# Gated mix of cached attention and a channel MLP, one decode step: four row groups and a float32 selector product in the output projection, first keys on a second DMA queue

## The chip, the core and the metric

The kernel runs on one core of a Trainium2 chip. A core has TensorE (PE; PEld is its weight load), VectorE (DVE), ScalarE (ACT), GpSimd (POOL) and SyncE (SP), and 16 DMA engines that all queues share. The metric is device time in microseconds, the median of several executions. One more execution is taken with the profiler; all profile times below are of that one.

## The reference

```python
def reference(A_x, A_k_cache, A_v_cache, A_wq, A_wo, B_x, B_w1, B_b1, B_w2, B_b2, gate_w):
    x = A_x                                                # (8, 1, 448) bf16
    g = _sigmoid((x * gate_w).sum(-1, keepdims=True))
    q = (x @ wq) -> 8 x 16 heads x 256                     # wq 448 x 4096
    k, v = the last 1024 rows of the caches (8, 8, 4096, 256), each head for 2 query heads
    a = (softmax(q k^T / 16) v) @ wo                       # wo 4096 x 448
    b = gelu(layernorm(x) @ w1 + b1) @ w2 + b2             # 448 -> 1792 -> 448
    return g * a + (1 - g) * b
```

## The kernel before

All data is bf16 in memory: 77.67 MB is read, nearly all of it the keys and values in use (8 batch rows, 4 MB of each), then `wq`, `w1`, `w2`, `wo`.

**Loads.** A ring of four 4 MB places (`RING = 4`) is filled in a planned order: keys of row 0, `wq`, keys 1, values 0, keys 2, values 1 and so on, `w1`, values 7 with `w2`, `wo`. `pump` issues a load when a place is free, `done` frees one. All these loads are issued by SP (`nc.sync`, lines 128, 140, 157). The keys of row 0 come in three pieces: two of 1 MB (`cuts` (2, 1)) and one of 2 MB. `wo` comes last, in seven pieces: chunks 0-7, 8-15, 16-19, 20-23, 24-27, 28-29 and 30-31 of its 32 chunks (one chunk is 128 rows of `wo`, 448 columns). Seven small loads (`x`, the gate weights, the biases) are issued by ScalarE.

**Pools.** Tiles come from pools. Tiles that are asked for under one tag share the pool's `bufs` places, and where no tag is given the tag is the name of the variable that the tile is bound to. When the places of a tag are taken, the next tile of that tag gets the place of an earlier one, and its first writer waits until the earlier one's readers have finished; a DMA that reads a tile has finished when it reports completion. `consts` has `bufs=1`. `ring`, `ktpool`, `epool`, `work` and `spool` are used with tags on purpose (`slot`, `kt`, `B`, ...).

**Stages.** The schedule is manual: every engine works in the order of the program text. `transpose_keys(b)` turns the 16 groups of four 128-column blocks of a row's keys, by TensorE (line 353) with a copy out of PSUM by ScalarE (groups in `BY_ACT`, line 359) or VectorE (line 361). For rows after 0 the first group goes another way: `turn_blocks` has one VectorE transpose (line 323) and 16 GpSimd copies (line 331). `between` hangs steps of the row before on single groups. `gate` computes the gate, `norm` the layer norm of x and its turned form, `query` the queries; then, for each row, `scores`, `top`, `expo`, `turn`, `scale`, `bring`, `values`, `finish`, `spread`. Row 0 runs as `transpose_keys(0); gate(); norm(); query(); scores(0); top(0)`. The turned x (`turned(0, ...)`), its statistics and the square root on ScalarE (lines 215 to 238) come ahead of all that.

**The end.** `mlp_hidden` gives the 14 weight chunks `hs` of the second MLP product. `oP` holds the attention output, 32 chunks. The output sum over 14 + 32 chunks is put together so: the 14 MLP chunks and chunks 0-7 go in turn to four row groups of `A1` (PSUM rows 0, 32, 64, 96; line 624), and four VectorE adds bring them into `acc` (line 632). Chunks 8-23 go to two row groups of `A3` (line 645), the odd ones up to 19 to `side`; one add brings the side in (line 653) and two bring in the rest as `fin` (line 657). The last eight chunks go to `A2`, each as two products of 224 columns in two row groups (line 666). One add gives `res`, 40 rows with both halves (line 673), and two output DMAs, one issued by SP and one by ScalarE, write one half each (lines 676, 677).

Of the kernel before, what the change touches and what calls it, by code (L numbers as in the profile page):

```python
# [17 lines left out]
def kernel(  # L18
# [27 lines left out]
    QD = 4  # L46
# [15 lines left out]
    CB = 4  # L62
    UR = NG * rep
    HALF = D // 2
    J8 = Dh // BL
    NQW = Hq // QD
    HS = NCK * Dh
    SLOT = NG * HS
    RING = 4
    EARLY = 8  # L70
    SIDE = 20
    TAIL = 8
    qscale = float(Dh) ** -0.5

    xf = A_x.rearrange("b s d -> (b s) d")
# [37 lines left out]
    def kv_loader(src, b, cuts=(1, 1), inner=False):  # L113
        pieces = [
            (i, k, cuts[i])
            for i in range(NG)
            for k in range(cuts[i])
        ]
        if inner:
            pieces.sort(key=lambda x: x[1])  # L120

        def load(t):
            for i, k, m in pieces:
                v = src[b, i * QD : (i + 1) * QD, kv_base:Sk, :].rearrange(
                    "a (s c) d -> s a (c d)", c=NCK
                )
                n = HS // m
                nc.sync.dma_start(
                    t[:, i * HS + k * n : i * HS + (k + 1) * n],
                    v[:, :, k * n : (k + 1) * n],  # L130
                )

        return load
# [71 lines left out]
    E = consts.tile([P, W + BL], F32)  # L205
    nc.gpsimd.memset(E[:, W:], 0.0)
    nc.gpsimd.memset(xs[1][:], 0.0)
    acc = consts.tile([NB, D], F32)
    fin = consts.tile([2 * BL, HALF], F32)
    nc.gpsimd.memset(fin[:], 0.0)  # L210
    oP = consts.tile([P, J8, NQW, NB], BF16)

    def turned(a, src):
# [13 lines left out]
                xw[BL * i : BL * (i + 1), a, :, BL : BL + NB], xt[:, :, i, 0:NB]  # L227
            )

    turned(0, x_sb[:])  # L230
    stats = consts.tile([NB, nc.vector.BN_STATS_DIM], F32)
    nc.vector.bn_stats(stats[:], x_sb[:])
    mv = consts.tile([NB, nc.vector.BN_AGGR_DIM], F32)
    nc.vector.bn_aggr(mv[:], stats[:])
    eps_t = consts.tile([NB, 1], F32)
    nc.vector.memset(eps_t[:], 1e-5)
    rstd = consts.tile([NB, 1], F32)
    nc.scalar.activation(rstd[:], mv[:, 1:2], ACT.Sqrt, bias=eps_t[:], scale=1.0)

    perm = consts.tile([P, P], BF16)  # L240
    mask = consts.tile([P, QD, rep], F32)
    gall = consts.tile([P, NB], F32)
    oall = consts.tile([P, NB], F32)
    b2s = consts.tile([NB, D], F32)
    b1_b = consts.tile([P, FQ], BF16)

    def gate():
        bc = consts.tile([BL, 2, D], BF16)
        nc.vector.stream_shuffle(
            bc[:].rearrange("p a d -> p (a d)"),  # L250
            rows_r[:].rearrange("p a d -> p (a d)"),
            [0] * BL,
        )
        prod = consts.tile([NB, D], F32)
        gl = consts.tile([NB, 1], F32)
        nc.vector.scalar_tensor_tensor(
            prod[:],
            in0=x_sb[:],
            scalar=1.0,
            in1=bc[0:NB, 0, :],  # L260
            op0=ALU.mult,
            op1=ALU.mult,
            accum_out=gl[:],
        )
        gth = consts.tile([NB, 1], F32)
        nc.scalar.activation(gth[:], gl[:], ACT.Tanh, scale=0.5)
        nc.vector.tensor_copy(
            perm[:].rearrange("p (s a) -> p s a", a=QD),
            ident[:].rearrange("p (a s) -> p s a", a=QD),
        )  # L270
        for r in range(rep):
            nc.vector.reduce_sum(
                mask[:, :, r], ident[:].rearrange("p (s a) -> p a s", a=QD), axis=AXIS.X
            )
        g32 = consts.tile([BL, BL], F32)
        nc.vector.memset(g32[:], 0.0)
        nc.vector.tensor_scalar(
            g32[0:NB, 0:1], gth[:], 0.5, 0.5, op0=ALU.mult, op1=ALU.add
        )
        om = consts.tile([NB, 1], F32)  # L280
        nc.vector.tensor_scalar(om[:], gth[:], -0.5, 0.5, op0=ALU.mult, op1=ALU.add)
        gt = consts.tile([BL, BL], F32)
        nc.vector.transpose(gt[:], g32[:])
        gb = consts.tile([BL, BL], F32)
        nc.vector.stream_shuffle(gb[:], gt[:], [0] * BL)
        for i in range(QD):
            nc.vector.tensor_copy(gall[BL * i : BL * (i + 1), :], gb[:, 0:NB])
        nc.vector.tensor_scalar(oall[:], gall[:], -1.0, 1.0, op0=ALU.mult, op1=ALU.add)
        nc.vector.tensor_scalar_mul(b2s[:], bc[0:NB, 1, :], om[:])

    def norm():
        nc.vector.reciprocal(rstd[:], rstd[:])
# [43 lines left out]
    def transpose_keys(b, between=None):  # L336
        between = between or {}
        kn = slot("k", b)[:].bitcast(F32)
        for hh in range(NG):
            kt = ktpool.tile([P, QD, NCK, SK, NJ], BF16, tag="kt", name="kt")  # L340
            KT[hh] = kt
            for i in range(NCK // CB):
                g = hh * (NCK // CB) + i
                if g == 0 and b > 0:
                    turn_blocks(kn, kt, 0)
                    for step in between.get(g, ()):
                        step()
                    continue
                ktp = ps_kt.tile([P, CB, P, NJ], BF16, tag="ktp", name="ktp")
                words = ktp[:].bitcast(F32)  # L350
                for c in range(CB):
                    o = (hh * NCK + i * CB + c) * P
                    nc.tensor.transpose(  # L353
                        words[:, c, :, 0], kn[:, o : o + P], ident_f[:]
                    )
                dst = kt[:, :, i * CB : (i + 1) * CB, :, :]
                src = ktp[:].rearrange("p c (s a) t -> p a c s t", a=QD)
                if g in BY_ACT:
                    nc.scalar.copy(dst, src)  # L359
                else:  # L360
                    nc.vector.tensor_copy(dst, src)  # L361
                for step in between.get(g, ()):
                    step()
        done()
# [208 lines left out]
    def steps(b):  # L573
# [8 lines left out]
        if b >= 1:  # L582
            d[9] = [lambda: finish(b - 1)]
            d[12] = [lambda: spread(b - 1)]
        return d

    transpose_keys(0)
    gate()
    norm()
    query()  # L590
    scores(0)
    top(0)
    for b in range(1, NB):
# [14 lines left out]
    spread(b)  # L608

    A1 = ps_misc.tile([P, D], F32, tag="misc", name="A1")  # L610
    A2 = ps_kt.tile([2 * BL, HALF], F32, tag="ktp", name="A2")
    A3 = ps_kt.tile([P, D], F32, tag="ktp", name="A3")
    nc.vector.memset(A2[:], 0.0)
    w2 = slot("w12")
    w = slot("wo")
    NCH = NQW * J8
    early = [(hs[:, c, :], w2[:, OW2 + c * D : OW2 + (c + 1) * D]) for c in range(FB)]
    chunks = [
        (oP[:, c % J8, c // J8, :], w[:, c * D : (c + 1) * D]) for c in range(NCH)
    ]  # L620
    early += chunks[0:EARLY]
    for i, (lhsT, rhs) in enumerate(early):
        g = i % QD
        nc.tensor.matmul(
            A1[BL * g : BL * g + NB, :],
            lhsT=lhsT,
            rhs=rhs,
            start=(i < QD),
            stop=(i >= len(early) - QD),
        )  # L630
    for g in range(QD):
        nc.vector.tensor_tensor(
            acc[:],
            A1[BL * g : BL * g + NB, :],
            acc[:] if g else b2s[:],
            op=ALU.add,
        )
    LAST = NCH - TAIL
    side = [c for c in range(EARLY, SIDE) if c % 2]
    main = [c for c in range(EARLY, LAST) if c not in side]  # L640
    res = consts.tile([2 * BL, HALF], BF16)
    for c in range(EARLY, LAST):
        mine, base = (side, 2 * BL) if c in side else (main, 0)
        lhsT, rhs = chunks[c]
        nc.tensor.matmul(  # L645
            A3[base : base + NB, :],
            lhsT=lhsT,
            rhs=rhs,
            start=(c == mine[0]),
            stop=(c == mine[-1]),  # L650
        )
        if c == side[-1]:
            nc.vector.tensor_tensor(
                acc[:], A3[2 * BL : 2 * BL + NB, :], acc[:], op=ALU.add
            )
    for h in range(2):
        nc.vector.tensor_tensor(
            fin[BL * h : BL * h + NB, :],
            A3[0:NB, h * HALF : (h + 1) * HALF],
            acc[:, h * HALF : (h + 1) * HALF],  # L660
            op=ALU.add,
        )
    for c in range(LAST, NCH):
        lhsT, rhs = chunks[c]
        for h in range(2):
            nc.tensor.matmul(  # L666
                A2[BL * h : BL * h + NB, :],
                lhsT=lhsT,
                rhs=rhs[:, h * HALF : (h + 1) * HALF],
                start=(c == LAST),  # L670
                stop=(c == NCH - 1),
            )
    nc.vector.tensor_tensor(
        res[0 : BL + NB, :], A2[0 : BL + NB, :], fin[0 : BL + NB, :], op=ALU.add
    )
    nc.sync.dma_start(out_f[:, 0:HALF], res[0:NB, :])
    nc.scalar.dma_start(out_f[:, HALF:D], res[BL : BL + NB, :])

# [1 line left out]
_INS = ['A_x', 'A_k_cache', 'A_v_cache', 'A_wq', 'A_wo', 'B_x', 'B_w1', 'B_b1', 'B_w2', 'B_b2', 'gate_w']  # L680
# [26 lines left out]
```

## Time and profile before

| | us |
|---|---|
| three runs | 194.12, 194.34, 194.59 (median 194.34) |
| the profiled execution | 194.37 |
| its span in the trace | 192.6 |
| PE / PEld / DVE / ACT / POOL busy | 121.0 / 77.1 / 111.0 / 90.4 / 47.9 |
| data moved, mean rate | 77.85 MB, 404 GB/s |

The span runs from the first to the last instruction; 1.8 us of the profiled execution lie around it. In a row such as "L645 PE MATMUL A<-slot,oP 128*8 128x448 bf16 x16", the line of the kernel, the engine, the operation, output and inputs, the weights' shape (128 rows, 8 columns), the moving operand's shape and the count follow each other. PEclk is the granted clock of TensorE, 1.00 being full. `A` stands for `A1`, `A2` and `A3`, since numbers are left out of names.

### The profile page before, as it was taken

The page shows a single profiled execution, that of the slowest core. Times are in us where ns is not written, and L with a number is a line of the kernel's source. Part 1 is how long each engine was busy: PE and PEld are TensorE (multiplying, and loading weights), DVE is VectorE, ACT ScalarE, POOL GpSimd, SP SyncE. Part 2 cuts the span into 40 slices and gives each one's busy share as a digit, 9 for nine tenths or more (in the row PEclk, how much of TensorE's full clock was granted, in tenths as well). Part 3 has the DMA queues.
Part 4 walks back from the last instruction along what each step waited for, and adds up shares of the span by engine and source line. Part 5 has one row for each costly group of instructions (what it writes and reads, how often), then busy time and mean ns, then how long its engine had stood idle before and what let it go on. Part 6 is the DMA issues. An engine that isn't in the chain of part 4 may idle for free.

```text
span 192.6 us, 2876 instructions
## 1 busy us (share of the span) xinstructions
PE 121.0 (63%) x1100; PEld 77.1 (40%) x1100; DVE 111.0 (58%) x251; ACT 90.4 (47%) x102; POOL 47.9 (25%) x125
## 2 busy tenths in 40 slices
PE   0768306679875598638773787667656793263582
PEld 0755103465662186318631674256316551010121
DVE  7615994864785068605870587068703876756532
ACT  2289400695994059425952585259422972010000
POOL 6000000480750066006700570048004900000000
PEclk9999855999999669996999789699975999755555
DMA  5999999999999999999999999999999999999960
GB/s 199 443 402 422 439 422 427 432 425 412 429 429 432 425 436 419 412 429 425 436 432 432 425 405 432 429 436 420 425 432 412 429 421 412 415 432 412 410 261 2
DMA packets 7128, 77.85 MB, mean 404 GB/s; under 512 B 830, under 2 KB 1228, under 8 KB 1996
## 3 DMA queue, kind: packets, MB, share of 16 engines
q1 hardware_dynamic: 7072, 77.67, 95.9%
q8 instruction: 8, 0.13, 0.3%
q14 instruction: 4, 0.03, 0.0%
q10 hardware_dynamic: 44, 0.02, 0.0%
HBM read 77.67 MB, written 0.01 MB: 403 GB/s over the span
## 4 chain that ended last, share of the span: by engine, by line
DMA 60%; PE 16%; DVE 14%; ACT 5%; issue 2%; DVEq 0%; ACTq 0%
DMA slot<-in_A_k_cache_dram 36%; DMA slot<-in_B_w_dram 14%; DMA slot<-in_A_wo_dram 10%; PE ktp L353 9%; ACT kt L359 5%; DVE kt L361 3%; PE S_ps L420 3%; PE A L645 2%; DVE qw L412 1%; DVE EB L444 1%; DVE EZ L455 1%; PE PO L491 1%; PE A L666 1%; DVE sc L453 1%; DVE nmx L433 1%
## 5 line engine op out<-in xcount | busy, mean ns | idle before, releaser
L359 ACT COPY kt<-ktp 128x1024 bf16<-128x1024 bf16 x80 | 76.3, 1023 | 37.0 <-PE ktp L353 36.8
L353 PE MATMUL ktp<-ident_f,slot 128*128 128x128 f32 x484 | 71.0, 300 | 28.9 <-DMA slot<-in_A_k_cache_dram 20.4
L353 PEld LDWEIGHTS ktp<-ident_f,slot 128*128 128x128 f32 x484 | 59.4, 154 | 47.6 <-issue 22.9
L331 POOL COPY kt<-B 32x128 f32<-32x128 f32 x112 | 44.8, 400 | 105.5 <-DVE B L323 101.2
L361 DVE COPY kt<-ktp 128x1024 bf16<-128x1024 bf16 x41 | 28.3, 689 | 19.0 <-PE ktp L353 18.9
L491 PE MATMUL PO<-slot,ET 128*16 128x512 bf16 x256 | 19.6, 455 | 16.6 <-DMA slot<-in_A_v_cache_dram 16.6
L323 DVE STREAM_TRANSPOSE B<-slot 128x512 f32<-128x512 f32 x7 | 5.0, 710 | 29.9 <-DMA slot<-in_A_k_cache_dram 29.9
L420 PE MATMUL S_ps<-kt,qw 128*4 128x512 bf16 x256 | 17.4, 412 | 7.3 <-DVE qw L412 7.3
L437 ACT ACTIVATE E<-S_ps,nmx 128x1024 f32<-128x1024 f32 x8 | 8.9, 1114 | 26.7 <-DVE nmx L433 26.7
L491 PEld LDWEIGHTS <-ET 128*16 128x16 bf16 x256 | 6.3, 97 | 28.4 <-DMA slot<-in_A_v_cache_dram 21.4
L433 DVE TENSOR_REDUCE nmx<-S_ps 128x1 f32<-128x1024 f32 x8 | 9.8, 1225 | 10.6 <-PE S_ps L420 10.6
L420 PEld LDWEIGHTS <-qw 128*4 128x4 bf16 x256 | 6.6, 85 | 15.5 <-DVE qw L412 8.1
L444 DVE STREAM_TRANSPOSE EB<-E 128x1056 f32<-128x1056 f32 x8 | 10.2, 1271 | 1.3 <-ACT E L437 1.3
L517 DVE TENSOR_TENSOR oP<-Y 32x32 bf16<-32x32 f32 x32 | 9.4, 294 | 1.1
L474 DVE TENSOR_TENSOR ET<-sm,mask 128x512 bf16<-128x512 f32 x8 | 5.5, 691 | 2.2 <-PE sm L466 2.1
L504 DVE STREAM_TRANSPOSE T<-PO 128x512 f32<-128x512 f32 x8 | 5.7, 708 | 1.6 <-PE PO L491 1.5
L466 PE MATMUL sm<-EZ,perm 128*128 128x128 bf16 x8 | 1.7, 216 | 6.3 <-DVE EZ L455 6.3
L559 ACT ACTIVATE zb<-za 128x448 f32<-128x448 f32 x1 | 0.6, 576 | 10.8 <-DVE za L558 10.8
L645 PE MATMUL A<-slot,oP 128*8 128x448 bf16 x16 | 4.1, 569 | 2.0 <-DMA slot<-in_A_wo_dram 1.3
L509 DVE TENSOR_TENSOR Y<-T 64x64 f32<-64x64 f32 x16 | 3.7, 234 | 0.6
L455 DVE TENSOR_TENSOR EZ<-EB,sc 128x128 bf16<-128x128 f32 x8 | 3.8, 472 | 0.3
L412 DVE COPY qw<-qt 32x64 bf16<-32x64 bf16 x16 | 3.3, 206 | 0.3
(88 smaller groups left out, 54.5 us busy)
## 6 DMA issues: line engine op xcount, KB each, us to landing
slot<-in_A_k_cache_dram SPq DMA_DIRECT2D x15, 2048.0 KB, 29.8
slot<-in_A_v_cache_dram SPq DMA_DIRECT2D x14, 2048.0 KB
slot<-in_A_v_cache_dram SPq DMA_DIRECT2D x4, 1024.0 KB, 23.6
slot<-in_A_wq_dram SPq DMA_DIRECT2D x3, 1024.0 KB
slot<-in_A_k_cache_dram SPq DMA_DIRECT2D x2, 1024.0 KB, 7.0
slot<-in_A_wo_dram SPq DMA_DIRECT2D x2, 896.0 KB
slot<-in_B_w_dram SPq DMA_DIRECT2D x1, 1568.0 KB
slot<-in_B_w_dram SPq DMA_DIRECT2D x1, 1344.0 KB
```

The costliest lines, as they stand in the source:

```text
L331: nc.gpsimd.tensor_copy(words[BL * w : BL * (w + 1), :, c0 : c0 + CB, g * S8 : (g + 1) * S8, 0], B[BL * g : BL * (g + 1), :, w].rearrange( ...
L353: nc.tensor.transpose(words[:, c, :, 0], kn[:, o : o + P], ident_f[:])
L359: nc.scalar.copy(dst, src)
L361: nc.vector.tensor_copy(dst, src)
L420: nc.tensor.matmul(S_ps[BL * t : BL * t + UR, n * QN : (n + 1) * QN], lhsT=qw[:, j, b, t, rep * u : rep * u + UR], rhs=KT[u][:, t, n * CQ ...
L433: nc.vector.reduce_max(nmx[:], S_ps[:], axis=AXIS.X, negate=True)
L437: nc.scalar.activation(E[:, 0:W], S_ps[:], ACT.Exp, bias=soft.pop(b)[:], scale=1.0, accum_out=E[:, W : W + 1],)
L444: nc.vector.transpose(EB[:].rearrange("p c r -> p (c r)"), E[:])
L455: nc.vector.tensor_tensor(EZ[:], EB[:, 0:NCK, 0:UR], sc[:].rearrange("p (o r) -> p o r", o=1).to_broadcast([P, NCK, UR]), op=ALU.mult,)
L491: nc.tensor.matmul(PO[BL * t : BL * t + Hq], lhsT=ET[:, c].rearrange("p u a r -> p (u a r)"), rhs=vn[:, c], start=(c < QD), stop=(c >= NCK ...
L517: nc.vector.tensor_tensor(oP[BL * i : BL * (i + 1), :, :, b], Yv[0:BL, :, :, i], Yv[BL : 2 * BL, :, :, i], op=ALU.add,)
L645: nc.tensor.matmul(A3[base : base + NB, :], lhsT=lhsT, rhs=rhs, start=(c == mine[0]), stop=(c == mine[-1]),)
```

## The change

Five things change. (1) The first 1 MB piece of the keys of row 0 is issued by ScalarE, ahead of the seven small loads there. (2) For row 0, too, the first group of keys is turned by `turn_blocks`. (3) The turned x and its statistics (`moments`) run after group 7 of row 0's keys, and `norm` runs after group 14 of row 2's keys. (4) All chunks but the last four go to four row groups of one PSUM tile `A1`, which one VectorE add with `b2s` brings to `accs`, 128 rows in float32; the last four chunks go to `A2` as four products of 112 columns in four row groups; ahead of the last two of them, four float32 products with the selector `pick` (128 rows, 8 columns: the sum of the four identity blocks' first eight columns) add the four row groups of `accs` into `A2`. (5) The output is copied out of `A2` in four copies of 8 x 112, two by VectorE into one `res` tile and two by ScalarE into another `res` tile, and each tile has its output DMA.

```diff
-    EARLY = 8
-    SIDE = 20
-    TAIL = 8
+    TAIL = 4
+    LATE = 2
...
-                nc.sync.dma_start(
+                eng = nc.scalar if (m, k, inner) == (2, 0, False) else nc.sync
+                eng.dma_start(
                     t[:, i * HS + k * n : i * HS + (k + 1) * n],
                     v[:, :, k * n : (k + 1) * n],
                 )
...
-    acc = consts.tile([NB, D], F32)
-    fin = consts.tile([2 * BL, HALF], F32)
-    nc.gpsimd.memset(fin[:], 0.0)
+    b2s = consts.tile([P, D], F32)
+    nc.gpsimd.memset(b2s[:], 0.0)
+    accs = consts.tile([P, D], F32)
...
-    turned(0, x_sb[:])
     stats = consts.tile([NB, nc.vector.BN_STATS_DIM], F32)
-    nc.vector.bn_stats(stats[:], x_sb[:])
...
+    def moments():
+        turned(0, x_sb[:])
+        nc.vector.bn_stats(stats[:], x_sb[:])
+        nc.vector.bn_aggr(mv[:], stats[:])
+        nc.scalar.activation(
+            rstd[:], mv[:, 1:2], ACT.Sqrt, bias=eps_t[:], scale=1.0
+        )
...
+        nc.vector.reduce_sum(
+            pick[:],
+            ident[:].rearrange("p (g b) -> p b g", g=QD)[:, 0:NB, :],
+            axis=AXIS.X,
+        )
...
-                if g == 0 and b > 0:
+                if g == 0:
                     turn_blocks(kn, kt, 0)
...
+        if b == 1:
+            d[14] = [norm]
         return d
-    transpose_keys(0)
+    transpose_keys(0, {7: [moments]})
     gate()
-    norm()
     query()
...
     A1 = ps_misc.tile([P, D], F32, tag="misc", name="A1")
-    A2 = ps_kt.tile([2 * BL, HALF], F32, tag="ktp", name="A2")
-    A3 = ps_kt.tile([P, D], F32, tag="ktp", name="A3")
-    nc.vector.memset(A2[:], 0.0)
+    A2 = ps_kt.tile([P, DO], F32, tag="ktp", name="A2")
+    nc.vector.memset(A1[:], 0.0)
...
+    wide, narrow = chunks[:-TAIL], chunks[-TAIL:]
+    for i, (lhsT, rhs) in enumerate(wide):
         g = i % QD
         nc.tensor.matmul(
             A1[BL * g : BL * g + NB, :],
             lhsT=lhsT,
             rhs=rhs,
             start=(i < QD),
-            stop=(i >= len(early) - QD),
-        )
...
+            stop=(i >= len(wide) - QD),
+        )
+    nc.vector.tensor_tensor(accs[:], A1[:], b2s[:], op=ALU.add)
+    narrow.insert(TAIL - LATE, (pick[:], accs[:]))
+    for i, (lhsT, rhs) in enumerate(narrow):
+        for t in range(QD):
             nc.tensor.matmul(
-                A2[BL * h : BL * h + NB, :],
+                A2[BL * t : BL * t + NB, :],
                 lhsT=lhsT,
-                rhs=rhs[:, h * HALF : (h + 1) * HALF],
-                start=(c == LAST),
-                stop=(c == NCH - 1),
-            )
-    nc.vector.tensor_tensor(
-        res[0 : BL + NB, :], A2[0 : BL + NB, :], fin[0 : BL + NB, :], op=ALU.add
-    )
-    nc.sync.dma_start(out_f[:, 0:HALF], res[0:NB, :])
-    nc.scalar.dma_start(out_f[:, HALF:D], res[BL : BL + NB, :])
+                rhs=rhs[:, t * DO : (t + 1) * DO],
+                start=(i == 0),
+                stop=(i == TAIL),
+            )
+    for h, (eng, copy) in enumerate(
+        ((nc.sync, nc.vector.tensor_copy), (nc.scalar, nc.scalar.copy))
+    ):
+        res = consts.tile([NB, 2, DO], BF16)
+        for i in range(2):
+            t = 2 * h + i
+            copy(res[:, i, :], A2[BL * t : BL * t + NB, :])
+        eng.dma_start(
+            out_f[:, h * HALF : (h + 1) * HALF], res[:].rearrange("b i d -> b (i d)")
+        )
```

`DO` is 112, a quarter of the 448 columns.

More of the change, by code (lines that the diff above doesn't have):

```diff
@@ L64 @@
     HALF = D // 2
+    DO = D // QD
     J8 = Dh // BL
@@ L228, in turned @@
             )
-    turned(0, x_sb[:])
     stats = consts.tile([NB, nc.vector.BN_STATS_DIM], F32)
-    nc.vector.bn_stats(stats[:], x_sb[:])
     mv = consts.tile([NB, nc.vector.BN_AGGR_DIM], F32)
-    nc.vector.bn_aggr(mv[:], stats[:])
     eps_t = consts.tile([NB, 1], F32)
@@ L237 @@
     rstd = consts.tile([NB, 1], F32)
-    nc.scalar.activation(rstd[:], mv[:, 1:2], ACT.Sqrt, bias=eps_t[:], scale=1.0)
     perm = consts.tile([P, P], BF16)
@@ L243 @@
     oall = consts.tile([P, NB], F32)
-    b2s = consts.tile([NB, D], F32)
+    pick = consts.tile([P, NB], F32)
     b1_b = consts.tile([P, FQ], BF16)
+    def moments():
[5 more added lines that the diff above has]
+        )
     def gate():
@@ L288, in gate @@
         nc.vector.tensor_scalar(oall[:], gall[:], -1.0, 1.0, op0=ALU.mult, op1=ALU.add)
-        nc.vector.tensor_scalar_mul(b2s[:], bc[0:NB, 1, :], om[:])
+        nc.vector.tensor_scalar_mul(b2s[0:NB, :], bc[0:NB, 1, :], om[:])
     def norm():
@@ L616 @@
     NCH = NQW * J8
-    early = [(hs[:, c, :], w2[:, OW2 + c * D : OW2 + (c + 1) * D]) for c in range(FB)]
     chunks = [
[L619 to L622, printed above, removed]
+        (hs[:, c, :], w2[:, OW2 + c * D : OW2 + (c + 1) * D]) for c in range(FB)
+    ] + [(oP[:, c % J8, c // J8, :], w[:, c * D : (c + 1) * D]) for c in range(NCH)]
+    wide, narrow = chunks[:-TAIL], chunks[-TAIL:]
+    for i, (lhsT, rhs) in enumerate(wide):
         g = i % QD
@@ L628 @@
             start=(i < QD),
-            stop=(i >= len(early) - QD),
+            stop=(i >= len(wide) - QD),
         )
-    for g in range(QD):
-        nc.vector.tensor_tensor(
[L633 to L636, printed above, removed]
-        )
[L638 to L650, printed above, removed]
-        )
-        if c == side[-1]:
-            nc.vector.tensor_tensor(
-                acc[:], A3[2 * BL : 2 * BL + NB, :], acc[:], op=ALU.add
-            )
[L656 to L661, printed above, removed]
-        )
@@ L663 @@
[L663 to L666, printed above, removed]
-                A2[BL * h : BL * h + NB, :],
-                lhsT=lhsT,
-                rhs=rhs[:, h * HALF : (h + 1) * HALF],
-                start=(c == LAST),
-                stop=(c == NCH - 1),
-            )
-    nc.vector.tensor_tensor(
-        res[0 : BL + NB, :], A2[0 : BL + NB, :], fin[0 : BL + NB, :], op=ALU.add
-    )
-    nc.sync.dma_start(out_f[:, 0:HALF], res[0:NB, :])
@@ L677 @@
-    nc.scalar.dma_start(out_f[:, HALF:D], res[BL : BL + NB, :])
+    nc.vector.tensor_tensor(accs[:], A1[:], b2s[:], op=ALU.add)
+    narrow.insert(TAIL - LATE, (pick[:], accs[:]))
+    for i, (lhsT, rhs) in enumerate(narrow):
+        for t in range(QD):
+            nc.tensor.matmul(
+                A2[BL * t : BL * t + NB, :],
+                lhsT=lhsT,
+                rhs=rhs[:, t * DO : (t + 1) * DO],
[11 more added lines that the diff above has]
+            out_f[:, h * HALF : (h + 1) * HALF], res[:].rearrange("b i d -> b (i d)")
+        )
```

## The prediction

> **What bounds the kernel now.** I read the page's slices first: does one resource run full all the way?
>
> ```profile
> PEclk9999855999999669996999789699975999755555
> DMA  5999999999999999999999999999999999999960
> GB/s 199 443 402 422 439 422 427 432 425 412 429 429 432 425 436 419 412 429 425 436 432 432 425 405 432 429 436 420 425 432 412 429 421 412 415 432 412 410 261 2
> ```
>
> The DMA engines are full from the first slice to slice 38 (a slice is 4.8 us). No engine is full, and TensorE ends at half clock. So 77.7 MB at some 424 GB/s set the time, and an edit can gain only where the stream starts or behind its end. The chain of waits, in order of time, shows the end:
>
> ```profile
> 164.12 18.72 DMA slot<-in_A_wo_dram
> ...
> 182.88 2.42 PE A L645 x12
> ...
> 185.33 0.63 DVE acc L653
> ...
> 186.00 0.68 PE A L645 x2
> ...
> 187.44 1.72 PE A L666 x6
> ...
> 189.19 0.38 DVE res L673
> ```
>
> After `wo`'s second piece (182.84) no transfer is on the chain: products in two row groups, an add that the next product waits for, products in one group, eight chunks in half products, an add. The windows and the timeline of the end say how far this trails the data:
>
> ```profile
> 185.00:186.00 1.00, 0.29 (x3) 0.08 (x2) 0.62 (x1) 0.00 (x0) 0.00 (x0) 0.50 0.72 271
> 186.00:187.00 1.00, 1.00 (x5) 0.34 (x5) 0.00 (x0) 0.00 (x0) 0.00 (x0) 0.50 0.45 163
> 187.00:189.60 2.60, 2.14 (x17) 1.02 (x14) 1.14 (x3) 0.00 (x0) 0.00 (x0) 0.50 0.00 0
> ```
>
> ```profile
> 180.66 0.92 PE L624 MATMUL A<-slot,oP 128*8 128x448 bf16 x8 [0.43 <-DMA slot<-in_A_wo_dram]
> ...
> 182.88 2.40 PE L645 MATMUL A<-slot,oP 128*8 128x448 bf16 x12 [1.30 <-DMA slot<-in_A_wo_dram]
> ...
> 187.07 2.06 PE L666 MATMUL A<-slot,oP 128*8 128x224 bf16 x14
> ...
> 189.19 0.38 DVE L673 TENSOR_TENSOR res<-A,fin 40x224 bf16<-40x224 f32 x1 [0.73 <-PE A L666]
> 189.60 0.37 SPq L676 DMA_DIRECT2D out_dram<-res  x1
> 189.60 0.30 ACTq L677 DMA_DIRECT2D out_dram<-res  x1
> ```
>
> The last columns of a window are clock, DMA share and GB/s: the stream is over at 187.0 and both output DMAs are issued at 189.60, 2.6 us later. Then SP's own waits:
>
> ```profile
> SPq L702 <- DMA out_dram<-res: 1.0, 1, 1.0
> ```
>
> SP begins this wait at 190.1 and leaves it at 191.06; the trace's completion records have SP's half at 191.04 and ScalarE's at 190.86. An output DMA thus takes 1.44 us (SP) or 1.25 us (ScalarE) from issue to completion. The span ends 1.55 us after the later one.
>
> **The change, part by part.** *Landings.* Pieces of 8 chunks land 2.2 us apart (180.66, 182.88), so four chunks take 1.1 us and two 0.55. A product waits for chunks 20-23 until 185.1; chunks 24-27 then land at 186.2, 28-29 at 186.8, 30-31 at 187.4.
>
> *Products and sum.* The 42 wide chunks in four groups keep up with this: at half clock four L624 products start together every 0.37 us, so eight chunks cost 0.75 against 2.2 between landings. Clearing `A1` (0.43, the row of L526 for the same shape) delays the MLP chunks from 178.6 to 179.7; they are done by 181.2 and chunks 0-7 by 182.0, before 182.8. The last four wide chunks start at 186.2 and end 0.53 later (shortest L645), 186.75. The add of 128 x 448 costs what L551 does (0.62, the same shape out of PSUM), with 0.05 for each handover: 187.42, `pick` starts at 187.47.
>
> *The float32 products.* No row has one on 8 columns. Low end: four bf16 products of 112 columns side by side, 0.09 (448 columns take 0.37). High end: four float32 products in turn at the rate of line 353 at half clock, in a window in which TensorE does nothing else:
>
> ```profile
> 68.00:70.00 2.00, 2.00 (x11) 2.00 (x11) 0.62 (x2) 1.01 (x1) 1.27 (x4) 0.50 0.96 410
> ```
>
> Eleven products in 2.0 us are 0.18 each, 0.73 for four. I take 0.37, the 448 columns in turn at bf16 pace: it lies midway and has float32 cost more than bf16, but without the 128-column weight load that line 353 carries. (The Trainium skill, FP8 and Floating Point Precision, TensorE Precision Notes, has true float32 make four passes through the array. By that, as an estimate, the four take 0.37 side by side and 1.49 in turn; with 1.49 the sum below would be 1.1 us higher. No run here shows it.) So 187.84; the last two chunks, landed by then, add 0.09 and a last product of 0.26 (L666 takes 0.35 on 224 columns, L645 0.53 on 448): the products end at 188.19 against 189.14 now.
>
> *The copies.* VectorE: adds out of PSUM take 0.62 on 448 and 0.38 on 224 columns, so 0.26 on 112; two with handover end at 188.75, and SP issues at 188.78 (now 189.60). To here the change is 0.8 us ahead. ScalarE's two copies, from its rows
>
> ```profile
> L359 ACT COPY kt<-ktp 128x1024 bf16<-128x1024 bf16 x80 | 76.3, 1023 | 37.0 <-PE ktp L353 36.8
> ...
> L559 ACT ACTIVATE zb<-za 128x448 f32<-128x448 f32 x1 | 0.6, 576 | 10.8 <-DVE za L558 10.8
> ```
>
> cost 0.23 + 0.78 ns per column, 0.32 each, 0.6 together. Beside VectorE they would end at 188.85. But the loop binds both tiles to the name `res`, in `consts`, which has one place per name. The second `res` gets the place of the first, so ScalarE's first copy must wait until the first tile's reader, SP's output DMA, has completed. In the code before, `res` was one tile and no writer waited for an output DMA. Queued behind the wait on ScalarE are its two copies and its output DMA, and nothing else; but the span's end waits for these. So: SP's issue 188.78 + 1.44 = 190.22; ScalarE's copies until 190.85; its DMA issued at 190.88, done 1.25 later at 192.13. Before it was 191.04: **+1.09**, less up to 0.2 because SP's last polls, 0.07 each, are partly past by then. I take +1.0. Bounds: the float32 products -0.3 to +0.4; copies 0.2 each instead of 0.3 (the shortest VectorE copies take 0.16) -0.3; a lone output DMA at 1.25 -0.2.
>
> *The start.* The page's first slice moves 199 GB/s; in half microsecond windows the stream has 229, 131 and 393 GB/s from 2.0 on, and 410 over 2.8 to 4.8. About 0.5 us are lost in the ramp. A second queue could fill at most that hole: between 0 and -0.4, below nothing since a first piece may come later; I take -0.1, nearer to nothing, because the same DMA engines carry both queues and the queue is full from 2.8 on. (The Trainium skill, DMA: Bandwidth & Descriptors, Issuing engines are not separate DMA queues, speaks against this part: it says that issuing from several engines saves sequencer time alone. By that the gain is nothing.)
>
> *Moves that I cost at nothing.* The first piece shares the engines with the second and lands near 7.6 instead of 5.8; x and the biases sit behind it. `turn_blocks` for row 0 is 0.71 on VectorE and 16 x 0.40 = 6.4 on an idle GpSimd. `moments` puts 3.1 us of VectorE (lines 215 to 234) and a 1.28 us table load with a 0.29 us root on ScalarE between row 0's groups; ScalarE's groups 8 to 15 queue behind the root, and the keys' place comes free some 1 to 2 us after 18.3. `norm`'s 3.5 us leave the path to the queries and go to 57-61 us, where they delay `top(2)` by about 1 us, ahead of idle VectorE at 62-66. `pick` adds one 0.27 reduction. The cover is the queue: by 14 us keys 0, `wq`, keys 1 and values 0 are issued, 16.2 MB, which last until 2.7 + 38 = 41 us, and SP's next load is issued at 18.3. Delays below 20 us cost nothing; without the backlog each would cost its full length. Scores of row 0 start 1 to 2 us sooner and gain nothing.
>
> Sum: +1.0 - 0.1 = +0.9 on the profiled execution's 194.37, 0.03 above the median of 194.34: **195.2**.
>
> **The rivals.** *No shared place* (or the wait is not there): both output DMAs issue by 188.88, 0.72 sooner, and with the start 193.5. The rows speak for it as they do for all but the wait; against it are one name and one buffer. Faster. 8%. *The wait is there but short*: cheap float32 products, copies at 0.2 and a completion of 1.25 take 0.8 of the 1.0, the start up to 0.3 more: 194.0 to 194.7. 14%, mostly within the bound of no change. *The float32 products run in turn, several times as long*: TensorE is in order, so the last two chunks and everything behind them move; 0.7 to 1.1 on top: 195.9 to 196.3. From 0.37 + 0.8 on this alone eats the lead of the products. Slower. 13%. *The head starves the queue*: the place of keys 0 would have to stay taken past 39 us instead of 18.3; nothing in the profile comes near. 2%.
>
> **How the numbers follow.** The forecast has 63%, its own range 194.7 to 195.8. Below 194.5 lie the first rival and half of the second, 15%, above 196.1 about 5%: range 194.5 to 196.1. A measurement of this kernel tells 0.2%, 0.39 us, from no change. Faster: the first rival and a little of the second, 0.10. Same: most of the second, 0.11. Slower: the rest, 0.79.
>
> **What would show it.** Right: ScalarE's copies of `res` start only after a wait of about 1.4 us on the output DMA, some 2 us after VectorE's; the output DMAs issue 2 us apart instead of together; the last product ends near 188.2; DMA windows are full from 3 to 185 us. Wrong: the copies on both engines start together (first rival), a gap of over 0.7 us between the add to `accs` and the last chunks (third), or a hole in the DMA row before 185 (fourth).

## The result and the profile after

The changed kernel takes **197.44 us** (median of six runs) against 194.47 for the kernel before on the same chip: ratio 1.0139, interval 1.0106 to 1.0173, so by the ratio 2.7 us slower. The forecast was slower, by 0.9: the direction held, and the time lies 1.3 us above the range's upper end of 196.1. The profiled execution has a span of 195.4 against 192.6.

The rows that answer to those shown of before, first the page's slices:

```profile
PEclk9999996699999999975999799999975799655555
DMA  5969999999999999999999999999999999999940
GB/s 213 444 234 397 438 429 424 426 429 429 426 421 429 429 429 417 429 429 429 423 429 429 429 423 429 426 429 414 429 429 426 429 426 412 416 436 413 406 174 3
```

The third slice has 6 tenths and 234 GB/s where the kernel before had 9 and 402. This is the hole that the prediction's last rival named and gave 2%. Windows of the changed kernel around it (busy time of the engines, clock, DMA share, GB/s):

```profile
5.00:10.00 5.00, 0.00 (x0) 0.00 (x0) 0.00 (x0) 0.00 (x0) 0.00 (x0) 1.00 1.05 446
...
12.00:16.00 4.00, 4.00 (x18) 3.67 (x19) 1.29 (x2) 3.33 (x4) 3.04 (x8) 1.00 0.53 157
```

From 12 to 16 us the stream carries 157 GB/s; the kernel before has 408 there:

```profile
12.00:16.00 4.00, 2.19 (x19) 1.98 (x19) 0.69 (x1) 3.18 (x4) 0.00 (x0) 1.00 0.97 408
```

The difference, 251 GB/s over 4 us, is 1.0 MB or 2.4 us of stream at 424 GB/s. Summed over windows from 2 to 20 us the changed kernel is 0.87 MB behind, 2.1 us. No engine is busy from 5 to 10 us either; work on the keys begins at 11.9. The timeline and SP's waits say why:

```profile
0.73 1.28 SPq L129 DMA_DIRECT2D slot<-in_A_k_cache_dram  x2
...
11.89 0.71 DVE L333 STREAM_TRANSPOSE B<-slot 128x512 f32<-128x512 f32 x1 [8.35 <-DMA slot<-in_A_k_cache_dram]
...
12.98 2.04 SPq L141 DMA_DIRECT2D slot<-in_A_wq_dram  x4
```

```profile
SPq L141 <- DMA x_sb<-in_A_x_dram: 11.0, 1, 11.0
```

The kernel before issues `wq` here:

```profile
6.35 2.01 SPq L140 DMA_DIRECT2D slot<-in_A_wq_dram  x4
```

The first piece of keys, issued by ScalarE at 0.73, is there at 11.9 instead of 5.8. x, behind it on the same queue, comes still later (complete at 12.96 by the trace's completion records), and SP's first load of `wq`, whose place in the ring was free from the start, waits 11.0 us for x; experiment 5 shows why it waits for x at all. It is issued at 12.98 (before: 6.35). Until then only the 4 MB of keys 0 are queued, and by about 12 us they have been moved.

The second loss stands in the timeline of the end:

```profile
188.10 0.54 PE L633 MATMUL A<-slot,oP 128*8 128x448 bf16 x4 [0.56 <-DMA slot<-in_A_wo_dram]
...
188.69 0.62 DVE L640 TENSOR_TENSOR accs<-A,b2s 128x448 f32<-128x448 f32 x1 [7.11 <-PE A L633]
...
189.37 0.56 PE L644 MATMUL A<-accs,pick 128*8 128x112 f32 x8 [0.35 <-DVE accs L640]
...
189.71 0.41 PE L644 MATMUL A<-slot,oP 128*8 128x112 bf16 x8
190.14 0.56 DVE L657 CAST res<-A 8x112 bf16<-8x112 f32 x2 [0.83 <-PE A L644]
190.73 0.36 SPq L658 DMA_DIRECT2D out_dram<-res  x1
192.06 0.50 ACT L657 CAST res<-A 8x112 bf16<-8x112 f32 x2 [17.00 <-DMA out_dram<-res]
192.59 0.31 ACTq L658 DMA_DIRECT2D out_dram<-res  x1
```

The last wide products start at 188.10 (the prediction had 186.2; the 1.9 us between are the hole). From there on all goes nearly as it was worked out, the wait of ScalarE's copies on SP's output DMA included: the releaser in the brackets is `out_dram<-res`, and the two output DMAs are issued 1.86 us apart.

### The profile page after: what moved, and what is told of

It is laid out like the page before. It is cut to its first block, busy times and chain, and to the rows that moved or that the text cites. A ratio compares the mean times of both kernels' runs of the same rounds, so it can differ in the third digit from the quotient of the medians.

```text
span 195.4 us, 2907 instructions
## 1 busy us (share of the span) xinstructions
PE 119.2 (61%) x1108; PEld 76.7 (39%) x1108; DVE 108.1 (55%) x247; ACT 91.7 (47%) x105; POOL 54.5 (28%) x141
## 4 chain that ended last, share of the span: by engine, by line
DMA 84%; PE 9%; ACT 3%; SPq 1%; issue 1%; DVE 0%; DVEq 0%; ACTq 0%
DMA slot<-in_A_v_cache_dram 69%; DMA slot<-in_A_wo_dram 8%; DMA slot<-in_A_k_cache_dram 6%; PE ktp L363 4%; PE PO L501 4%; ACT kt L369 2%; SPq L129 1%; PE S_ps L382 1%; ACT L248 1%; DMA out_dram<-res 1%; PE S_ps L394 1%; PE A L644 0%; DVE accs L640 0%; PE A L633 0%; ACT res L657 0%
## 5 line engine op out<-in xcount | busy, mean ns | idle before, releaser
L363 PE MATMUL ktp<-ident_f,slot 128*128 128x128 f32 x480 | 71.9, 304 | 34.7 <-DMA slot<-in_A_k_cache_dram 25.7
L363 PEld LDWEIGHTS ktp<-ident_f,slot 128*128 128x128 f32 x480 | 60.0, 156 | 53.6 <-issue 29.3
L341 POOL COPY kt<-B 32x128 f32<-32x128 f32 x128 | 51.2, 400 | 100.9 <-DVE B L333 95.9
L371 DVE COPY kt<-ktp 128x1024 bf16<-128x1024 bf16 x40 | 27.5, 687 | 16.8 <-PE ktp L363 16.5
L501 PE MATMUL PO<-slot,ET 128*16 128x512 bf16 x256 | 18.9, 442 | 15.3 <-DMA slot<-in_A_v_cache_dram 15.3
L333 DVE STREAM_TRANSPOSE B<-slot 128x512 f32<-128x512 f32 x8 | 5.7, 710 | 35.4 <-DMA slot<-in_A_k_cache_dram 35.4
L657 ACT CAST res<-A 8x112 bf16<-8x112 f32 x2 | 0.5, 245 | 17.0 <-DMA out_dram<-res 17.0
L640 DVE TENSOR_TENSOR accs<-A,b2s 128x448 f32<-128x448 f32 x1 | 0.6, 623 | 7.1 <-PE A L633 7.1
```

The costliest lines, as they stand in the source:

```text
L333: nc.vector.transpose(B[:].rearrange("p c w s a -> p (c w s a)"), kn[:, c0 * P : (c0 + CB) * P],)
L341: nc.gpsimd.tensor_copy(words[BL * w : BL * (w + 1), :, c0 : c0 + CB, g * S8 : (g + 1) * S8, 0], B[BL * g : BL * (g + 1), :, w].rearrange( ...
L363: nc.tensor.transpose(words[:, c, :, 0], kn[:, o : o + P], ident_f[:])
L501: nc.tensor.matmul(PO[BL * t : BL * t + Hq], lhsT=ET[:, c].rearrange("p u a r -> p (u a r)"), rhs=vn[:, c], start=(c < QD), stop=(c >= NCK ...
```

## The experiments

**1. Two places for the output tiles.**

```diff
-        res = consts.tile([NB, 2, DO], BF16)
+        res = consts.tile([NB, 2, DO], BF16, tag=f"res{h}", name="res")
```

> The changed kernel, but the two output tiles have places of their own. Theory (the end costs what the shared place costs): in the changed kernel ScalarE's copies start 1.85 us after VectorE's first copy is done, because they wait for SP's output DMA; without the wait they start beside VectorE's, near 190.1, and ScalarE's output DMA issues near 190.8 instead of 192.6. The last completion moves from 193.9 to 192.2: 1.7 us less than the changed kernel's 197.4, so about 195.7, and the hole in the stream at 12.5 to 15.5 us is still there. Rival (the end is slow because of the float32 products and narrow copies, not because of the wait): at most 0.3 us less, 197.1 or more.

Measured: 196.05, ratio 1.0078 (1.0048 to 1.0108) to the kernel before; 1.4 us less than the changed kernel's median, 1.2 by the two ratios. The hole is still there (161 GB/s from 12 to 16 us), and SP issues at 190.72, as in the changed kernel (190.73). The theory holds, but of its 1.7 us 0.3 were missing, and the timeline names a wait that it did not have:

```profile
190.13 0.56 DVE L657 CAST res<-A 8x112 bf16<-8x112 f32 x2 [0.83 <-PE A L644]
...
190.78 0.50 ACT L657 CAST res<-A 8x112 bf16<-8x112 f32 x2 [16.11 <-DVE res L657]
191.31 0.30 ACTq L658 DMA_DIRECT2D out_dram<-res  x1
```

ScalarE's copies now wait for VectorE's: the releaser in the brackets is `DVE res`. Both read the one PSUM tile `A2`, and the program has them do so in turn, though on different rows. Experiments 7 and 10 take this wait away.

**2. The first keys on SP again.** The moved steps stay.

```diff
-                eng = nc.scalar if (m, k, inner) == (2, 0, False) else nc.sync
+                eng = nc.sync
```

> The changed kernel, but the first keys are issued by SP again; the moved steps (moments, norm, the first group of row 0 by VectorE and GpSimd) stay. Theory (the second queue makes the hole: x lands behind the first keys, and the first load of wq waits for x's completion count): no hole at 12.5 to 15.5 us, wq issued near 6.4, the last data near 187.4 instead of 189.0: 1.6 to 1.7 us less than 197.4, so about 195.7. Rival (the moved steps hold the queue): the hole stays, 197.4.

Measured: 195.41, ratio 1.0042 (1.0020 to 1.0065), 2.0 us less than the changed kernel's median, 1.9 by the two ratios. There is no hole (406 GB/s from 12 to 16 us), `wq` is issued from 6.76 on. The moved steps alone make no hole. What is left, 0.8 us over the kernel before, is the prediction's own case, the shared place without the hole:

```profile
188.25 0.56 DVE L657 CAST res<-A 8x112 bf16<-8x112 f32 x2 [0.83 <-PE A L644]
188.84 0.37 SPq L658 DMA_DIRECT2D out_dram<-res  x1
190.17 0.50 ACT L657 CAST res<-A 8x112 bf16<-8x112 f32 x2 [17.38 <-DMA out_dram<-res]
190.70 0.30 ACTq L658 DMA_DIRECT2D out_dram<-res  x1
```

**3. Both repairs.**

> Both repairs: two places for the output tiles and the first keys on SP. Theory (two independent costs, the rest of the change is the gain that the prediction worked out for it): 197.4 - 1.7 - 1.65 = 194.0 to 194.1, 0.3 to 0.4 under the kernel before; by the sum of the prediction without its wait 193.6. Rival (the costs overlap, one hides the other): 195 or more.

Measured: 194.10, ratio 0.9979 (0.9962 to 0.9995). The two costs add up.

**4. One part alone on the kernel before: the first keys on ScalarE's queue.**

```diff
-                nc.sync.dma_start(
+                eng = nc.scalar if (m, k, inner) == (2, 0, False) else nc.sync
+                eng.dma_start(
```

> The kernel before with one part of the change: the first keys issued by ScalarE, ahead of x. Theory: the hole comes from this part alone, so it shows here too, near 12.5 to 15.5 us, with the first load of wq issued near 13 instead of 6.4; the stream ends 1.6 to 2.1 us later: 196.0 to 196.5. Rival (the hole needs the moved steps): no hole, within 0.4 us of the kernel before.

Measured: 196.14, ratio 1.0091 (1.0055 to 1.0126), 1.8 us slower. SP waits for x again, and `wq` is issued at 12.95:

```profile
SPq L141 <- DMA x_sb<-in_A_x_dram: 10.9, 1, 10.9
```

So this one part makes the hole, and the moved steps have no share in it.

**5. x ahead of the keys on ScalarE's queue.** Is it x's place in the queue, or that `wq` waits for whichever load holds its semaphore?

```diff
-    pump()
     nc.scalar.dma_start(x_sb[:], xf)
+    pump()
```

> The changed kernel, with x loaded by ScalarE ahead of the first keys instead of behind them. Theory A (it is the order of the load semaphores: eight serve all loads in turn, so the first load of wq waits for the third load that was issued, whichever that is; with x first, the third is the piece of keys on ScalarE's queue): x lands near 2 us, but wq still waits until that piece lands, near 11 to 12 us, so the hole is there and shorter by some 1 us: 196.2 to 197.2. Theory B (only x behind the keys matters): wq issued before 7 us, no hole, 195.7.

Measured: 196.66 (two runs), ratio 1.0104 (1.0070 to 1.0138). x is early now, yet `wq` is issued at 12.98 all the same, and SP's longest wait at line 141 is for keys:

```profile
SPq L141 <- DMA slot<-in_A_k_cache_dram: 16.1, 3, 10.9
```

Theory A holds. A semaphore is a counter that a load raises when it completes; an issue that takes a semaphore again waits until the load that had it last is complete. In the traces the loads of SP and ScalarE take eight semaphores in turn, and the first load of `wq` has the third one. In the changed kernel x had it; with x first, the late piece of keys has it. The hole is not shorter, since that piece, issued second, was complete only at 12.96.

**6. The small loads on GpSimd.** Their loads count on semaphores of their own, so `wq` follows nothing that is late; the first keys stay on ScalarE's queue.

```diff
-    nc.scalar.dma_start(x_sb[:], xf)
+    nc.gpsimd.dma_start(x_sb[:], xf)
...
```

(and so for the other six)

> The changed kernel, with the seven small loads issued by GpSimd, whose loads have semaphores of their own, and the first keys still by ScalarE. Theory A: wq's loads now wait for nothing that is late, SP issues them by 5 us, there is no hole although the first keys still come late: 1.6 to 2.0 us under the changed kernel, 195.4 to 195.8, with the end (shared place) still in it. Rival (a second queue of keys itself slows the stream): 196.5 or more, with DMA windows below 400 GB/s between 5 and 15 us.

Measured: 195.50, ratio 1.0046 (1.0029 to 1.0064). SP's timeline:

```profile
2.06 2.25 SPq L141 DMA_DIRECT2D slot<-in_A_wq_dram  x4
4.35 8.20 SPq L129 DMA_DIRECT2D slot<-in_A_k_cache_dram  x2
```

`wq` is issued from 2.06 on and the stream has no hole, although the first keys still finish near 12 us. The late keys alone cost nothing that can be told; the wait of `wq` costs. Beside experiment 2 (1.0042) the second queue itself shows no gain.

**7. A PSUM tile for each half**, on top of both repairs.

```diff
-    A2 = ps_kt.tile([P, DO], F32, tag="ktp", name="A2")
+    A2 = [ps_kt.tile([P, DO], F32, tag="ktp", name="A2") for _ in range(2)]
...
-                A2[BL * t : BL * t + NB, :],
+                A2[t // 2][BL * t : BL * t + NB, :],
...
-            copy(res[:, i, :], A2[BL * t : BL * t + NB, :])
+            copy(res[:, i, :], A2[h][BL * t : BL * t + NB, :])
```

> As the kernel with both repairs, but each half of the last chunks has a PSUM tile of its own. There ScalarE's first copy waits for VectorE's second one, which reads the same PSUM tile: 188.99 against 188.35. Theory: this wait is the 0.5 us that kernel lies above the sum of the prediction; without it ScalarE copies from 188.35, both output DMAs issue near 188.9, 0.6 earlier than 189.53: 193.5. Rival (SP's output DMA, issued at 188.93 and slower to complete, ends the span anyway): at most 0.4 us less, 193.7 or more.

Measured: 193.85, ratio 0.9955 (0.9937 to 0.9973). By the median this is the rival's 193.7 or more; by the ratio, on the 194.37 of before that stood beside both repairs, it is the theory's 193.5. So the run does not decide between them. In its profiled execution the last data came 2.4 us late, so experiment 10 repeats it.

**8. The new end alone on the kernel before**, with two places for the output tiles and one PSUM tile.

> The kernel before with the new end alone, with two places for the output tiles (first keys, moments, norm and row 0's first group as before). Theory (the moved steps are hidden by the queue, as the prediction has it): the same as the kernel with both repairs, 193.9 to 194.2, with the last data at the same 187.4. Rival (the moved steps cost or gain by themselves): over 0.4 us away from that.

Measured: 194.35, ratio 0.9995 (0.9975 to 1.0015), a little above the theory's 193.9 to 194.2. The last data are complete at 187.35, as with both repairs (187.40). Within its interval this is the kernel with both repairs (0.9979): that `moments`, `norm` and row 0's first group were moved makes no difference that can be told. Nor can the new end with one PSUM tile, by this run alone, be told from the kernel before.

**9 and 10. Two ways out, side by side.** The ninth keeps the first keys on ScalarE's queue, with the small loads on GpSimd, two places and two PSUM tiles; the tenth is experiment 7 again.

> The changed kernel whole, first keys on ScalarE's queue included, with its waits taken away instead: the seven small loads on GpSimd, two places for the output tiles, a PSUM tile for each half. Theory: all three costs are gone, 193.4 to 193.6, with the stream near 187.1 as where only the small loads moved. Rival (the second queue gains nothing): the same as with the first keys on SP, 193.5 to 193.9.

> The kernel with first keys on SP, two places for the output tiles and a PSUM tile for each half, again, beside the other: 193.5 to 193.9. In its first profiled execution (196.06) one DMA engine was 2.4 us behind the rest at the end; theory: that is of the execution, not of the kernel, so the last piece of wo lands near 187.4 here and the output DMAs issue near 188.9.

Measured: 193.85, ratio 0.9981 (0.9965 to 0.9997), and 193.60, ratio 0.9974 (0.9952 to 0.9996). Both lie under the kernel before by 0.2 to 0.3%, with intervals that end just below 1, and far under the changed kernel; between them the second queue shows no gain. The theory of the ninth (193.4 to 193.6) is missed, its rival holds. The end of the tenth:

```profile
188.30 0.54 DVE L657 CAST res<-A 8x112 bf16<-8x112 f32 x2 [0.83 <-PE A L644]
188.34 0.50 ACT L657 CAST res<-A 8x112 bf16<-8x112 f32 x2 [15.32 <-PE A L644]
188.87 0.36 SPq L658 DMA_DIRECT2D out_dram<-res  x1
188.87 0.30 ACTq L658 DMA_DIRECT2D out_dram<-res  x1
```

Both engines copy at once, released by TensorE, and both output DMAs are issued at 188.87, 0.73 earlier than in the kernel before. By the completion records the last one is done at 190.29, against 190.74 with both repairs and one tile, and 191.0 in the kernel before. In the times of the runs the second tile is less clear: the intervals of the ratios with two tiles (0.9955, 0.9981, 0.9974) all overlap that of both repairs with one (0.9979).

## Why the prediction was wrong

*What bounds the kernel*: right. What the change costs came from a hole in the stream (1.9 us by the ratios of experiment 2 and the whole) and from behind the stream's end (0.8).

*Products, sum, float32 products*: right in time. In experiment 2, where the stream is undisturbed, the add starts at 186.80 (forecast 186.80) and VectorE's copies at 188.25 (188.24). The four float32 products hold the array for 0.34 us (189.37 to 189.71 in the changed kernel; 0.37 was taken). That the number fits is in part luck: 0.37 was taken as four products in turn, each at bf16 pace, but in the trace they run side by side. They stand as eight records, two each; the first four start within 0.02 us of each other, and the whole takes 0.335 us, 3.6 times the 0.094 of the four bf16 products behind it. The four-pass rule that the prediction quoted from the Trainium skill, FP8 and Floating Point Precision, TensorE Precision Notes, agrees with this for products side by side, 0.37 by that estimate; its in-turn case of 1.49, and with it the third rival, fell.

*The shared place*: right, within 0.2. SP issues at 188.84 (forecast 188.78), ScalarE's copies start at 190.17 (190.22 and a handover), its output DMA is issued at 190.70 (190.88). Two terms were too large: SP's output DMA, alone on its way, took 1.23 us to its completion record and not 1.44, and the copies 0.25 each, not 0.32. Experiment 2, the change without the second queue, measures +0.8 us, ratio 1.0042, where the forecast for the whole was +0.9. So the direction was no luck.

*The moves costed at nothing*: **this is the step that failed**, with 1.8 to 2.0 us (experiments 2 and 4, one undoing the part and one doing it alone). Two sentences of it were wrong. "The first piece shares the engines with the second and lands near 7.6": it was done at 11.9. And "by 14 us keys 0, `wq`, keys 1 and values 0 are issued" was taken from the kernel before as if SP's issues depended on free places alone. They also wait in turn for completions of earlier loads, and the change put x, on which `wq` waits, behind the late piece. Either error alone would have cost little: with the piece at 7.6, as an estimate that no run tests, `wq` would have been issued near 8, with keys 0 lasting until about 12; with the piece at 11.9 and no wait there is no hole (experiment 6). The profile of before held the clue: among SP's own waits there, from 0 to 16 us, its loads wait for completions of keys and `wq`,

```profile
SPq L128 <- DMA slot<-in_A_k_cache_dram: 6.8, 2, 3.7
SPq L128 <- DMA slot<-in_A_wq_dram: 1.9, 1, 1.9
```

and its third load was issued at 5.78, the moment the first was complete. The prediction's fourth rival asked only whether the place of keys 0 stays taken, not which completion an issue waits for.

*The start*: the gain of 0.1 did not come. Experiments 2 and 6, and 9 and 10, differ by less than their intervals. That agrees with the rule that the prediction quoted from the Trainium skill, DMA: Bandwidth & Descriptors, Issuing engines are not separate DMA queues, that a second issuing engine saves issue time only. The runs add that the piece moved to the second queue came 6 us later (11.9 against 5.8).

*No shared place* (193.5): with the places apart and the keys on SP it was 194.1. The two engines' copies of one PSUM tile go in turn, which the working did not have; with two tiles it was 193.85 and 193.60 (experiments 7 and 10), and the output DMAs were issued at 188.87, where this rival had 188.88.

## What to carry to other kernels

When a transfer moves to another queue, list for every later issue what it waits for, free places and completion counts both, and follow each back to the transfer that moved: a full queue hides a late load, but not an issue that waits for it. A name that a loop binds again gives its tiles one place in a pool with one buffer, and a tile read by an output DMA holds its place until that DMA completes; at the end of this kernel that cost 1.2 to 1.4 us (experiment 1 beside the changed kernel, experiment 3 beside 2). Two engines that empty one PSUM tile did it in turn here (copies from 188.34 and 188.99 in experiment 3); two tiles let them run side by side (188.30 and 188.34 in experiment 10).

## What the runs showed of the hardware

- Of two loads issued at 0.73 us by SP and ScalarE, ScalarE's 1 MB began at 4.66 in the changed kernel, when 112 of the 128 packets of SP's first 1 MB had started, and from 5.9 to 10.9 us the two queues' packets alternated, 16 KB of SP's next load against 8 KB. In the records of the changed kernel, and of experiments 5 and 6, the last packet of this piece ended at 10.9 to 12.0. That the queues alternate by packet is read from these records; why SP's first load went ahead nearly whole stays open.
- Two output DMAs of 3.5 KB issued at once took 1.25 (ScalarE) and 1.44 us (SP) from issue to completion in the kernel before, 1.24 and 1.42 in experiment 10. Issued apart, in experiment 2, each took 1.22 to 1.23, and the wait on SP's was over 1.33 us after its issue.
- In the kernel before, products of line 666 start at 186.33 and 186.70, ahead of the last products of line 645 at 187.07, which stand before them in the program: products of different row groups of the output overtake each other in the records. In these rows, then, products start in order only within a row group, where the third rival had TensorE in order throughout.
